# Queries projected with tokens on partitions and turned by DMA, 19 of 20 features a head, and a gram with the keys stationary

## The chip, the cores and the metric

The kernel runs on one core of a Trainium2 chip. The metric is device time in microseconds (us) of one execution. Beside the timed runs there is one profiled execution of the kernel, whose span runs from its first to its last instruction. The core has a matrix engine (TensorE, PE in the profile, with PEld for its loads of stationary operands), a vector engine (DVE), a scalar engine (ACT), GpSimd (POOL), and SyncE (SP), which here only issues DMAs. Each engine runs its own instructions in order and waits on semaphores for the others.

## The reference

x is 2048 tokens by 640 features; there are 32 heads of 20 features. The output mixes a linear attention, whose feature map is a softmax over the 20 features of a head and a softmax of the negated values, with a GEGLU feed-forward of width 1728. The sizes and the function:

```python
    def _A_ref(x, wqkv, w_phi, wo):
...
        qkv = (lambda x, *d: x.transpose(*d))((x @ wqkv).reshape(B, S, 3, H, Dh), 2, 0, 3, 1, 4)
        q, k, v = qkv[0], qkv[1], qkv[2]
        pq = jnp.einsum("bhsd,hdf->bhsf", q, w_phi)
        pk = jnp.einsum("bhsd,hdf->bhsf", k, w_phi)
        phi_q = jnp.concatenate([_softmax(pq, axis=-1), _softmax(-pq, axis=-1)], axis=-1)
        phi_k = jnp.concatenate([_softmax(pk, axis=-1), _softmax(-pk, axis=-1)], axis=-1)
        kv = jnp.einsum("bhsf,bhsd->bhfd", phi_k, v)
        z  = jnp.einsum("bhsf->bhf", phi_k)
        num = jnp.einsum("bhqf,bhfd->bhqd", phi_q, kv)
        den = jnp.einsum("bhqf,bhf->bhq", phi_q, z)[..., None] + 1e-6
        o = num / den
        return (lambda x, *d: x.transpose(*d))(o, 0, 2, 1, 3).reshape(B, S, D) @ wo

    def _B_ref(x, w_gate, w_up, w_down):
        return (_gelu(x @ w_gate) * (x @ w_up)) @ w_down

    x = A_x
    g = _sigmoid((x * gate_w).sum(-1, keepdims=True))
    a = _A_ref(x, A_wqkv, A_w_phi, A_wo)
    b = _B_ref(x, B_w_gate, B_w_up, B_w_down)
    return g * a + (1 - g) * b
```

## The kernel before

All work is written in one order by hand. A small recorder, `_Sched`, gives each operation to its engine in that order and puts in the waits: every operation names the buffers (keys) that it reads and writes, and waits for the last writer of what it reads and for the last writer and all readers of what it writes. A DMA counts as a reader of its source until it has landed. PE never waits for PE. The 16 lanes of SP's queue are used in turn, and a lane waits for its previous DMA.

The tokens are 16 tiles of 128 (`t`), in four blocks of 512 (`b`). The stages:

1. Loads. `loads` (line 208) issues everything on SP: x and the three parts of wqkv, partly by a transposing DMA, and then all feed-forward weights and wo (lines 247 to 257). POOL makes masks and the columns of ones of `vaug`.
2. Folding. `fold` (line 328) multiplies wk and wq by the block-diagonal w_phi, so that pk and pq come straight from x: six matmuls for each 128 rows, and one copy out of PSUM (DVE at line 354, ACT at line 356).
3. Attention state, `attention_state` (line 551). For each token tile: v and pk (`proj`, five matmuls for each stretch of columns, tokens on the partitions), the two exponentials of pk and the gate's exponential on ACT (`k_evac`, lines 423 and 426), the softmax sums, reciprocals and scaling on DVE (`k_norm`, lines 438, 447, 452), and `gram` (line 463), which adds the tile's keys-times-values to PSUM. In the gram the values, 64 columns for three heads, are stationary and 60 key features of both signs are moving; two groups of heads lie side by side in the two column halves of the array. The queries are made for a block of 512 tokens and 128 features at once (`pq`, line 530): the weights are stationary, the 512 tokens moving, so the features come out on the partitions, as the numerators need them; two exponentials (line 537) write them to `Eq`. With `self.columns` set, from the first gram on, `mm` (line 358) writes each matmul as two of 64 stationary columns. The loop over t from 4 to 15 is the main part: k and v of tile t, gram of earlier tiles, and some `pq` units of earlier blocks, in PSUM banks that alternate.
4. The state is turned: `kv_evac` (line 475) copies the gram out and turns it by a DMA (line 494), `kv_mask` (line 509) and `kv_ones` fill `KV`.
5. Feed-forward, `ffn` (line 786). `gateup` (line 640): per block and 128 hidden features, five matmuls of 512 tokens for the gate and five for the up part, gelu on ACT (line 653), product on DVE (line 655). PSUM pairs (0, 1) and (6, 7) alternate. The three last grams stand between the first gateups. `down_pair` (line 716) makes the output of two tiles, with the attention's part added through `goT`.
6. Numerators, `num` (line 671): for each token tile 20 matmuls of 88 columns (four heads), 64 rows each, two at a time in the two row halves of the array; then some small DVE operations, and a transposing DMA (line 713) to `goT`. Tiles 0 and 1 are done between gateups of block 1, the other 14 between downs.

Of the kernel before, what the change touches and what calls it, by code (L numbers as in the profile page):

```python
# [3 lines left out]
P = 128  # L4
# [103 lines left out]
class _Kernel:  # L108
# [13 lines left out]
    NSE = 4  # L122
    NSV = 8
# [8 lines left out]
    def run(self):  # L132
        nc = self.nc
        self.alloc()
        self.columns = False
        self.sc = _Sched(nc, {"sp": (nc.sync, 16), "act": (nc.scalar, 4), "pool": (nc.gpsimd, 2)})
        self.loads()
        self.attention_state()
        self.ffn()
        self.sc.finish(nc.sync)  # L140

    def alloc(self):
# [9 lines left out]
        self.Eq = T("Eq", [P, 2, KD, S], BF16)  # L152
        self.KV = T("KV", [P, KD, 2, self.HB * self.DB], BF16)
        self.hmask = T("hmask", [P, 2, KD, self.HB], BF16)
# [8 lines left out]
        self.hT2 = T("hT2", [P, NFC, BT], BF16)  # L163
        self.wphi_sb = T("wphi_sb", [P, KD, DH], BF16)

        def place(lists):
# [15 lines left out]
            for name, shape, dt, c in plans:  # L182
# [3 lines left out]
            [("w3", [P, KD, 2 * D + 2], BF16), ("wq2", [P, KD, D], BF16)],  # L186
# [3 lines left out]
            [("Ek", [P, self.NSE, 2, D], BF16), ("vaug", [P, self.NSV, self.H, self.DA], BF16),  # L190
             ("Dk", [P, self.NSE, 2, 2 * self.H], F32)],
# [3 lines left out]
            [("xtok", [P, self.TB, D], BF16), ("wkT", [P, KD, D], BF16), ("wqT", [P, KD, D], BF16)],  # L195
            [("goT", [P, 8, KD, P], BF16), ("O1", [P, 2, D], BF16), ("O2", [P, 2, D], BF16),
             ("Og", [P, 2, D], BF16), ("RH", [P, 2, 8, 2, 16], F32), ("outsb", [P, 4, D], BF16)],
# [10 lines left out]
    def loads(self):  # L208
# [34 lines left out]
        half = 7 * P  # L243
        g3 = self.wg.rearrange("(kt p) n -> p kt n", p=P)
        u3 = self.wu.rearrange("(kt p) n -> p kt n", p=P)
        for i, (a, b) in enumerate(((0, half), (half, 13 * P))):
            sc.dma("sp", lambda e, a=a, b=b: e.dma_start(self.wg_sb[:, :, a:b], g3[:, :, a:b]), writes=[("wg", i)])
            sc.dma("sp", lambda e, a=a, b=b: e.dma_start(self.wu_sb[:, :, a:b], u3[:, :, a:b]), writes=[("wu", i)])
            if i == 0:
                sc.dma("sp", lambda e: e.dma_start(self.wgu_sb[:, :, 0:64], g3[:, :, 13 * P:self.F]), writes=["wgu0"])  # L250
                sc.dma("sp", lambda e: e.dma_start(self.wgu_sb[:, :, 64:128], u3[:, :, 13 * P:self.F]), writes=["wgu1"])
        sc.dma("sp", lambda e: e.dma_start(self.wd_sb[:, 0:13, :],
                                           self.wd[0:13 * P, :].rearrange("(c p) n -> p c n", p=P)), writes=["wd"])
        for r in (0, 1):
            sc.dma("sp", lambda e: e.dma_start(self.wd_sb[64 * r:64 * r + 64, 13, :], self.wd[13 * P:self.F, :]),
                   writes=[("wd13", r)])
        sc.dma("sp", lambda e: e.dma_start(self.wo_sb[:, :, :], self.wo.rearrange("(kt p) n -> p kt n", p=P)),
               writes=["wo"])
# [18 lines left out]
        for r in (0, 1):  # L277
            m = self.hmask[:, r, :, :]
            pool(lambda e, m=m: e.memset(m, 1.0), [("hmask", r)])
            pool(lambda e, m=m, r=r: e.affine_select(  # L280
                m, m, pattern=[[4, KD], [-DH, self.HB]], compare_op=ALU.is_ge, fill=0.0, base=-64 * r,
                channel_multiplier=1), [("hmask", r)])
            pool(lambda e, m=m, r=r: e.affine_select(
                m, m, pattern=[[-4, KD], [DH, self.HB]], compare_op=ALU.is_ge, fill=0.0, base=DH - 1 + 64 * r,
                channel_multiplier=-1), [("hmask", r)])
        for s in range(self.NSV):
            pool(lambda e, s=s: e.memset(self.vaug[:, s, :, DH:self.DA], 1.0), [("vone", s)])

# [31 lines left out]
    def gate_column(self, b):  # L320
# [4 lines left out]
        sc.op("dve", lambda e: e.tensor_copy(self.w3[:, :, 2 * self.D:2 * self.D + 1], pv[:, 0:self.KD].unsqueeze(2)),  # L325
              reads=[("ps", b)], writes=["wgate"])

    def fold(self, kt, which, banks, ekey):
# [16 lines left out]
        src = self.pair(banks)  # L345
        if which == "k":
            dst = self.w3[:, kt, self.D:2 * self.D].rearrange("p (b c) -> p b c", c=320)
        else:
            dst = self.wq2[:, kt, :].rearrange("p (i r c) -> p r i c", r=2, c=64)
            src = src.rearrange("p r (i c) -> p r i c", c=64)  # L350
        rd = [("ps", b) for b in banks]
        wr = [("w%s2" % which, kt)]
        if ekey == "d":
            self.sc.op("dve", lambda e: e.tensor_copy(dst, src), reads=rd, writes=wr)
        else:
            self.sc.op("act", lambda e: e.activation(dst, src, AF.Copy), reads=rd, writes=wr)

    def mm(self, bank, c0, n, lhs, rhs, first, fin, reads):

        for a, z in ((0, 64), (64, P)) if self.columns else ((0, P),):  # L360
            self.sc.op("pe", lambda e: e.matmul(  # L361
                self.ps[a:z, bank * 512 + c0:bank * 512 + c0 + n], lhs[:, a:z], rhs, start=first, stop=fin),
                reads=reads, writes=[("ps", bank)], signal=fin and z == P)
# [27 lines left out]
    def k_early(self, t, b0):  # L391
        self.proj(t, 640, 384, b0, 128, ["wk2"])
        self.proj(t, 1024, 257, b0 + 1, 0, ["wk2", "wgate"])
        self.k_evac(t, b0)

    def v_early(self, t, b0):
        self.proj(t, 0, 512, b0, 0, ["wv"])
        self.proj(t, 512, 128, b0 + 1, 0, ["wv"])
        self.v_evac(t, b0)

    def vk(self, t):
        self.proj(t, 0, 512, 0, 0, ["wv"])
        self.proj(t, 512, 512, 1, 0, ["wv", "wk2"])
        self.proj(t, 1024, 257, 2, 0, ["wk2", "wgate"])
        self.v_evac(t, 0)
        self.k_evac(t, 1)

    def v_evac(self, t, B, ek="a"):
        sv = t % self.NSV
        if ek == "d":  # L410
            self.sc.op("dve", lambda e: e.tensor_copy(
                self.vaug[:, sv, :, 0:self.DH], self.bank(B, self.D).rearrange("p (h d) -> p h d", d=self.DH)),
                reads=[("ps", B), ("ps", B + 1), ("vone", sv)], writes=[("vaug", sv)])
            return
        self.sc.op("act", lambda e: e.activation(
            self.vaug[:, sv, :, 0:self.DH], self.bank(B, self.D).rearrange("p (h d) -> p h d", d=self.DH), AF.Copy),
            reads=[("ps", B), ("ps", B + 1), ("vone", sv)], writes=[("vaug", sv)])

    def k_evac(self, t, b0):
        se = t % self.NSE  # L420
        o = b0 * 512 + 128
        for s, scale in ((0, 1.0), (1, -1.0)):
            self.sc.op("act", lambda e, s=s, scale=scale: e.activation(  # L423
                self.Ek[:, se, s, :], self.ps[:, o:o + self.D], AF.Exp, scale=scale),
                reads=[("ps", b0), ("ps", b0 + 1)], writes=[("Ek", se, s)])
        self.sc.op("act", lambda e: e.activation(  # L426
            self.gcol[:, t:t + 1], self.ps[:, o + self.D:o + self.D + 1], AF.Exp, scale=-1.0),
            reads=[("ps", b0 + 1)], writes=[("gcol", t)])
# [5 lines left out]
    def k_sums(self, t):  # L434
        sc = self.sc
        se = t % self.NSE
        H, DH = self.H, self.DH
        sc.op("dve", lambda e: e.tensor_reduce(  # L438
            self.Dk[:, se, 0, :].rearrange("p (s h) -> p s h", h=H),
            self.Ek[:, se, :, :].rearrange("p s (h d) -> p s h d", d=DH), AX.X, ALU.add),  # L440
            reads=[("Ek", se, 0), ("Ek", se, 1)], writes=[("Dk", se)])

    def k_scale(self, t):
        sc = self.sc
        se = t % self.NSE
        H, DH = self.H, self.DH
        sc.op("dve", lambda e: e.reciprocal(self.Dk[:, se, 1, :], self.Dk[:, se, 0, :]),
              reads=[("Dk", se)], writes=[("Rk", se)])
        for s in (0, 1):
            v = self.Ek[:, se, s, :].rearrange("p (h d) -> p h d", d=DH)  # L450
            r = self.Dk[:, se, 1, s * H:(s + 1) * H].unsqueeze(2).to_broadcast([P, H, DH])
            sc.op("dve", lambda e, v=v, r=r: e.tensor_tensor(v, v, r, ALU.mult),  # L452
                  reads=[("Rk", se)], writes=[("Ek", se, s)])

    def gram_groups(self):

        fe = 3 * self.DH
        for g in range(11):
            u = g // 2
            yield (g, 64 * (g % 2), 3 + u // 4, 2 * fe * (u % 4), min(3 * g * self.DA, self.H * self.DA - 64), fe * g,  # L460
                   min(fe, self.D - fe * g))

    def gram(self, t):
        sc = self.sc
        se, sv = t % self.NSE, t % self.NSV
# [85 lines left out]
    def attention_state(self):  # L551
# [16 lines left out]
        for t in range(4):  # L568
            vs(t, 0)
# [305 lines left out]
```

## Time and profile before

| | us |
|---|---|
| median of 3 runs (286.4 to 286.93) | 286.66 |
| span of the profiled execution | 285.0 |
| PE busy in it | 281.1 |
| DVE busy | 174.4 |
| ACT busy | 105.2 |
| POOL busy | 5.3 |
| loads, first v tiles and folds | 0 to 25 |
| main loop and first gateups | 25 to 84 |
| gateups | 84 to 196 |
| downs, with 14 numerators | 196 to 283 |

The span of the profile is 1.7 us shorter than the median of the runs. "Busy" of PE counts a matmul until its result is out, though the next begins long before that, so a group's mean time of one matmul (379 ns for 512 columns) is not what one adds to the span; the distance between starts (216 ns) is.

### The profile page before, as it was taken

The numbers are of one execution on the slowest core, as the hardware profiler recorded it, in microseconds if no ns is written. First come the engines' busy times: TensorE is split into PE (matmuls) and PEld (weight loads), VectorE is DVE, ScalarE is ACT, GpSimd is POOL, SyncE is SP. The second block draws the span as 40 slices with busy tenths as digits, with TensorE's granted clock in tenths as the row PEclk, the third lists the DMA queues.
The fourth block names the chain that finished last, engine by engine and source line by source line (L and its number), as shares of the span: only waits on it lengthen the run. The fifth ranks groups of instructions, "written<-read, shape, count | busy, mean of one in ns | idle before, by whom it ended". The sixth has DMA issues, their size and how long they took to land.

```text
span 285.0 us, 7066 instructions
## 1 busy us (share of the span) xinstructions
PE 281.1 (99%) x3045; PEld 186.1 (65%) x3060; DVE 174.4 (61%) x352; ACT 105.2 (37%) x200; POOL 5.3 (2%) x36
## 2 busy tenths in 40 slices
PE   8999999999999999999999999999999999999996
PEld 4665799999984444444444444445777777777786
DVE  1459999999976652667242334225883883883801
ACT  4367898667754223222322223221112112112021
POOL 7000000000000000000000000000000000000000
DMA  8999993000002000011000000000233223322421
GB/s 228 225 199 313 361 349 111 2 0 2 2 0 48 0 0 2 2 23 25 0 0 0 2 0 0 0 2 0 26 82 58 50 62 59 70 52 68 71 72 48
DMA packets 36937, 18.67 MB, mean 66 GB/s; under 512 B 28970, under 2 KB 36394, under 8 KB 36906
## 3 DMA queue, kind: packets, MB, share of 16 engines
q1 hardware_dynamic: 36240, 18.19, 26.3%
q8 instruction: 24, 0.39, 0.6%
q10 hardware_dynamic: 666, 0.03, 0.2%
q14 instruction: 7, 0.06, 0.1%
HBM read 9.04 MB, written 2.62 MB: 41 GB/s over the span
## 4 chain that ended last, share of the span: by engine, by line
PE 99%; issue 0%; ACT 0%
PE ps L361 62%; PE ps L737 28%; PE ps L681 2%; PE ps L373 2%; PE ps L468 2%; PE ps L341 1%; PE ps L557 1%; PE ps L298 0%; ACT outsb L750 0%; PE ps L564 0%; PE ps L323 0%
## 5 line engine op out<-in xcount | busy, mean ns | idle before, releaser
L361 PE MATMUL ps<-xT,wg_sb 128*128 128x512 bf16 (+1 forms) x265 | 63.8, 379 | 0.4 <-issue 0.2
L361 PE MATMUL ps<-xT,wu_sb 128*128 128x512 bf16 (+1 forms) x263 | 63.3, 379 | 0.4
L653 ACT ACTIVATE gl<-ps 128x512 bf16<-128x512 f32 x52 | 30.9, 596 | 72.9 <-PE ps L361 70.7
L655 DVE TENSOR_TENSOR hT<-ps,gl 128x512 bf16<-128x512 f32 x39 | 26.6, 689 | 38.8 <-PE ps L361 38.7
L737 PE MATMUL ps<-wd_sb,hT 64*128 64x320 bf16 x648 | 48.5, 296 | 0.0
L361 PEld LDWEIGHTS ps<-xT,wu_sb 128*128 128x128 bf16 (+1 forms) x270 | 26.6, 99 | 29.5
L361 PEld LDWEIGHTS ps<-xT,wg_sb 128*128 128x128 bf16 (+1 forms) x270 | 26.2, 99 | 29.0 <-ACT gl L653 0.2
L361 PE MATMUL ps<-w,xT 128*64 128x512 bf16 (+6 forms) x398 | 41.5, 325 | 0.1
L750 ACT ACTIVATE outsb<-ps,Gm 128x320 bf16<-128x320 f32 (+2 forms) x31 | 14.5, 515 | 72.4 <-PE ps L737 72.4
L737 PEld LDWEIGHTS ps<-wd_sb,hT 64*128 64x128 bf16 x648 | 31.1, 94 | 12.2 <-issue 0.4
L361 PEld LDWEIGHTS ps<-w,xT 128*64 128x64 bf16 (+1 forms) x400 | 35.9, 107 | 4.5
L737 PE MATMUL ps<-wo_sb,goT 64*128 64x320 bf16 (+2 forms) x340 | 26.5, 288 | 0.0
L361 PE MATMUL ps<-xT,wq 128*64 128x512 bf16 (+1 forms) x184 | 26.0, 380 | 0.1
L438 DVE TENSOR_REDUCE Dk<-Ek 128x64 f32<-128x1280 bf16 x16 | 23.7, 1478 | 3.7 <-ACT gcol L426 3.7
L452 DVE TENSOR_TENSOR Ek<-Ek,Dk 128x640 bf16<-128x640 bf16 x32 | 25.0, 821 | 0.6
L708 DVE TENSOR_TENSOR O<-ps,RH 128x640 bf16<-128x640 f32 x32 | 24.7, 815 | 0.0
L423 ACT ACTIVATE Ek<-ps 128x640 bf16<-128x640 f32 x32 | 20.7, 703 | 4.2 <-PE ps L361 4.2
L537 ACT ACTIVATE Eq<-ps 128x512 bf16<-128x512 f32 x40 | 21.6, 607 | 0.6 <-PE ps L361 0.4
L655 DVE TENSOR_TENSOR xT<-ps,gl 128x512 bf16<-128x512 f32 x13 | 9.0, 690 | 18.2 <-PE ps L361 18.2
L737 PEld LDWEIGHTS ps<-wo_sb,goT 64*128 64x128 bf16 x340 | 16.0, 94 | 5.3
L361 PEld LDWEIGHTS ps<-xT,wq 128*64 128x64 bf16 (+1 forms) x185 | 15.4, 108 | 2.9
L737 PE MATMUL ps<-wd_sb,xT 64*128 64x320 bf16 (+2 forms) x270 | 16.0, 269 | 0.0
(71 smaller groups left out, 173.8 us busy)
## 6 DMA issues: line engine op xcount, KB each, us to landing
out_dram<-outsb SPq DMA_DIRECT2D x7, 320.0 KB, 2.3
wd_sb<-in_B_w_down_dram SPq DMA_DIRECT2D x1, 2080.0 KB, 12.9
wg_sb<-in_B_w_gate_dram SPq DMA_DIRECT2D x1, 1120.0 KB, 7.4
wu_sb<-in_B_w_up_dram SPq DMA_DIRECT2D x1, 1120.0 KB, 9.8
wg_sb<-in_B_w_gate_dram SPq DMA_DIRECT2D x1, 960.0 KB, 9.1
wu_sb<-in_B_w_up_dram SPq DMA_DIRECT2D x1, 960.0 KB, 9.3
w<-in_A_wqkv_dram SPq DMA_DIRECT2D x5, 160.0 KB, 3.6
wo_sb<-in_A_wo_dram SPq DMA_DIRECT2D x1, 800.0 KB, 8.5
```

The source lines that it names most:

```text
L361: self.sc.op("pe", lambda e: e.matmul(self.ps[a:z, bank * 512 + c0:bank * 512 + c0 + n], lhs[:, a:z], rhs, start=first, stop=fin), reads=r ...
L373: sc.op("pe", lambda e, c0=c0, n=n, bk=bk, col=col: e.matmul(self.bank(bk)[:, col:col + n], self.xT[:, kt, t * P:(t + 1) * P], self.w3[:, ...
L423: self.sc.op("act", lambda e, s=s, scale=scale: e.activation(self.Ek[:, se, s, :], self.ps[:, o:o + self.D], AF.Exp, scale=scale), reads=[ ...
L438: sc.op("dve", lambda e: e.tensor_reduce(self.Dk[:, se, 0, :].rearrange("p (s h) -> p s h", h=H), self.Ek[:, se, :, :].rearrange("p s (h d ...
L452: sc.op("dve", lambda e, v=v, r=r: e.tensor_tensor(v, v, r, ALU.mult), reads=[("Rk", se)], writes=[("Ek", se, s)])
L468: sc.op("pe", lambda e: e.matmul(self.ps[a:a + 64, b * 512 + c:b * 512 + c + 2 * nf], va[:, lo:lo + 64], self.Ek[:, se, :, f0:f0 + nf], st ...
L537: sc.op("act", lambda e, s=s, scale=scale: e.activation(self.Eq[:, s, i, b * self.BT:(b + 1) * self.BT], self.bank(bank), AF.Exp, scale=sc ...
L653: sc.op("act", lambda e: e.activation(self.gl[:, slot, :], self.bank(banks[0]), AF.Gelu_apprx_tanh), reads=[("ps", banks[0])], writes=[("g ...
L655: sc.op("dve", lambda e: e.tensor_tensor(hT, self.bank(banks[1]), self.gl[:, slot, :], ALU.mult), reads=[("ps", banks[1]), ("gl", slot)], ...
L708: dve(lambda e, o=o, f=f, s=s: e.tensor_tensor(o, V[s][:, :, :, 0:DH], f, ALU.mult), rb + [key(6 + s)], [("O", s, sl)], guard=old)
L737: sc.op("pe", lambda e: e.matmul(self.bank(bk, w), lhs, rhs, start=opens and x == 0, stop=end and not opens, skip_group_check=True), reads ...
L750: sc.op("act", lambda e: e.activation(dst, self.bank(bk, w), AF.Copy, scale=g), reads=rd, writes=wr)
```

## The change

The queries are now made as the keys are: one token tile at a time (`q_tile`), tokens on the partitions, 608 columns. Their exponentials go to a buffer `Eqt` of four slots (`NEQ = 4`, slot `t % 4`), and a transposing DMA on SP turns each tile into `Eq`, features on the partitions. Because a softmax does not change when one value is subtracted from all, the fold subtracts each head's last feature from the others: 19 columns a head are left (`E = 19`), the exponential of the twentieth is the constant 1, and the sums get 1 added. So k has 608 columns and not 640, and so has q; a `fold` now ends in a small ACT copy of the last features (`wref`) and a DVE subtraction. Three heads with both signs make one group of 128 features (60 and 4 unused, twice); there are 11 groups. In the gram the 128 key features of a group are stationary and 63 value columns are moving; the result has the features on the partitions already, so the state needs three masked DVE copies (`kv_state`) and no DMA. The numerators take 11 groups of three heads (66 columns), sign 0 in the upper and sign 1 in the lower row half. `self.columns` is gone. The constant columns of `Ek` and `Eqt` are set by nine POOL memsets at the start; per key tile a POOL copy puts the reciprocals in the twentieth columns. v of a tile is made four tiles ahead of its k. The feed-forward weights but the first halves of gate and up are issued from inside the main loop (`weights(1)` to `weights(6)`), behind the query tiles' DMAs on SP. `hT2` shares its memory with `Eqt`.

```diff
-    NSE = 4
-    NSV = 8
+    NSE = 5
+    NSV = 9
+    NEQ = 4
+    E = DH - 1
+    G = 11
+    HG = 3
+    VO = 167
+    KO = 208
...
-    def fold(self, kt, which, banks, ekey):
+    def fold(self, kt, which, banks):
...
+        self.sc.op("act", lambda e: e.activation(ref, src[:, :, :, self.E], AF.Copy), reads=rd, writes=[("wref", kt)])
+        self.sc.op("dve", lambda e: e.tensor_tensor(
+            dst, src[:, :, :, 0:self.E], ref.unsqueeze(3).to_broadcast([P, 2, 16, self.E]), ALU.subtract),
+            reads=rd + [("wref", kt)], writes=[("w%s2" % which, kt)])
+
+    def strip(self, b):
+
+        c = (b + 1) * 512 + 304
+        self.sc.op("dve", lambda e: e.memset(self.ps[:, c:c + self.E], 0.0), writes=[("ps", b + 1)])
...
+    def v_tile(self, t, b):
+        n = 512 - self.VO
+        self.proj(t, 0, n, b, self.VO, ["wv"])
+        self.proj(t, n, self.D - n, b + 1, 0, ["wv"])
...
+    def exps(self, T, sl, name, b):
+
+        o = b * 512 + self.KO
+        src = self.ps[:, o:o + self.G * self.HG * self.E].rearrange("p (g h f) -> p g h f", h=self.HG, f=self.E)
         for s, scale in ((0, 1.0), (1, -1.0)):
...
+            self.sc.op("act", lambda e: e.activation(dst, src, AF.Exp, scale=scale),
+                       reads=[("ps", b), ("ps", b + 1)], writes=[(name, sl, s)])
+
+    def k_tile(self, t, b):
+        n = 513 - self.KO
+        self.proj(t, self.D, n, b, self.KO - 1, ["wk2", "wgate"])
+        self.proj(t, self.D + n, self.H * self.E + 1 - n, b + 1, 0, ["wk2"])
+        self.exps(self.Ek, t % self.NSE, "Ek", b)
...
+    def q_tile(self, t, b):
+        n = 512 - self.KO
+        for bk, c0, a, z in ((b, self.KO, 0, n), (b + 1, 0, n, self.H * self.E)):
+            for kt in range(self.KD):
+                self.mm(bk, c0, z - a, self.xT[:, kt, t * P:(t + 1) * P], self.wq2[:, kt, a:z], kt == 0,
+                        kt == self.KD - 1, [("xT", t), ("wq2", kt)])
+        sl = t % self.NEQ
+        self.exps(self.Eqt, sl, "Eqt", b)
+        self.sc.dma("sp", lambda e: e.dma_start_transpose(self.Eq[:, :, t * P:(t + 1) * P], self.Eqt[:, sl, :]),
+                    reads=[("Eqt", sl, 0), ("Eqt", sl, 1)], writes=[("Eq", t)])
...
     def k_scale(self, t):
...
+        sc.op("dve", lambda e: e.tensor_scalar(D, D, 1.0, None, op0=ALU.add), reads=[("Dk", se)], writes=[("Dk", se)])
+        sc.op("dve", lambda e: e.reciprocal(R, D), reads=[("Dk", se)], writes=[("Rk", se)])
+        sc.op("pool", lambda e: e.tensor_copy(v[:, :, :, self.E], R3), reads=[("Rk", se)], writes=[("Ekc", se)])
+        sc.op("dve", lambda e: e.tensor_tensor(
+            v[:, :, :, 0:self.E], v[:, :, :, 0:self.E],
+            R3.unsqueeze(3).to_broadcast([P, 2 * self.G, self.HG, self.E]), ALU.mult),
+            reads=[("Rk", se)], writes=[("Ek", se, 0), ("Ek", se, 1)])
...
     def gram(self, t):
...
+        for g in range(self.G):
+            n, b, c = min(w, self.H * self.DA - w * g), 4 + g // 8, w * (g % 8)
+            self.sc.op("pe", lambda e: e.matmul(
+                self.bank(b)[:, c:c + n], self.Ek[:, se, g * P:(g + 1) * P], va[:, w * g:w * g + n],
...
     def attention_state(self):
...
+        f, v, k, q = self.fold, self.v_tile, self.k_tile, self.q_tile
+        v(4, 6)
+        v(5, 0)
+        f(0, "k", (2, 3))
+        f(1, "k", (4, 5))
+        f(2, "k", (6, 7))
+        v(6, 0)
+        f(3, "k", (2, 3))
+        f(4, "k", (4, 5))
+        v(7, 6)
+        self.strip(2)
+        k(0, 2)
+        self.strip(6)
+        f(0, "q", (4, 5))
+        f(1, "q", (0, 1))
+        k(1, 6)
+        self.k_sums(0)
+        f(2, "q", (4, 5))
+        k(2, 2)
+        f(3, "q", (0, 1))
+        f(4, "q", (4, 5))
+        self.strip(0)
+        k(3, 6)
         self.k_scale(0)
...
+        for t in (1, 2, 3):
+            self.k_norm(t)
+        g = 0
         for t in range(4, NT):
...
+            if t + 4 < NT:
+                v(t + 4, 0)
+            k(t, 2)
+            for g in range(g, t - 3 if t < 8 else t - 2):
+                self.gram(g)
+            g = t - 3 if t < 8 else t - 2
+            q(t - 4, 6)
             self.k_norm(t)
...
+            if t < 7:
+                self.weights(t - 3)
+            elif t in (9, 10, 11):
+                self.weights(t - 5)
+            if t + 4 >= NT:
+                q(t, 0)
...
     def num(self, t):
...
+        for g in range(self.G):
+            n = min(w, H * DB - w * g)
             for s in (0, 1):
...
+                a, o = 64 * s, base[s] + w * g
+                sc.op("pe", lambda e: e.matmul(
+                    self.ps[:, o:o + n], self.Eq[a:a + 64, g, t * P:(t + 1) * P], self.KV[a:a + 64, g, 0:n],
...
         def state(idx):
             if idx < 3:
                 self.gram(13 + idx)
             if idx == 2:
-                self.columns = False
-                self.kv_evac()
+                self.kv_state()
                 self.gates()
-                self.kv_ones()
-            if 6 <= idx < 11:
-                self.kv_mask(idx - 6)
```

`weights(4)` is w_down (2080 KB), `weights(5)` its last 64 rows in two DMAs, `weights(6)` wo (800 KB); they follow the query tiles 5, 6 and 7 on SP.

## The prediction

> **What bounds the kernel now.** I read the busy times, then the chain of work that ended last, then PE's waits, then the chain in order of time through the main loop.
>
> ```profile
> PE 281.1 (99%) x3045; PEld 186.1 (65%) x3060; DVE 174.4 (61%) x352; ACT 105.2 (37%) x200; POOL 5.3 (2%) x36
> ...
> PE 99%; issue 0%; ACT 0%
> PE ps L361 62%; PE ps L737 28%; PE ps L681 2%; PE ps L373 2%; PE ps L468 2%; PE ps L341 1%; PE ps L557 1%; PE ps L298 0%; ACT outsb L750 0%; PE ps L564 0%; PE ps L323 0%
> ```
>
> PE is the chain: 99% of it. What counts is the matmul columns it streams and every wait put before them. PE's own waits, all of them:
>
> ```profile
> PE ps L557 <- PEq L860: 0.8, 1, 0.8
> PE ps L361 <- issue: 0.2, 1, 0.2
> ```
>
> So nothing before makes PE wait. One round of the main loop, and the end of the grams:
>
> ```profile
> 60.26 0.22 PE ps L468 x7
> 60.48 0.05 PE ps L361
> 60.53 0.04 PE ps L468
> 60.56 3.73 PE ps L361 x34
> 64.30 0.27 PE ps L468 x8
> ...
> 83.93 0.35 PE ps L468 x10
> 84.28 0.16 issue
> ```
>
> A round is some 4.1 us, of which the gram is 0.31 (0.27 and a piece of 0.04). After the last gram PE goes from 64-column to 128-column operands and loses 0.16 and a little more. By the starts of single matmuls in the trace, 512 columns take 216 ns, 384 take 162, 257 take 109.5, 128 take 55.5: columns / 2.4 + about 2.4 ns. I use that formula below. The groups by shape (busy, mean ns of one, idle before) that the costs below are taken from:
>
> ```profile
> L452 DVE TENSOR_TENSOR Ek<-Ek,Dk 128x640 bf16<-128x640 bf16 x32 | 25.0, 821 | 0.6
> ...
> L361 PEld LDWEIGHTS ps<-xT,wu_sb 128*128 128x128 bf16 x250 | 24.5, 98 | 29.5
> ...
> L438 DVE TENSOR_REDUCE Dk<-Ek 128x64 f32<-128x1280 bf16 x16 | 23.7, 1478 | 3.7 <-ACT gcol L426 3.7
> ...
> L423 ACT ACTIVATE Ek<-ps 128x640 bf16<-128x640 f32 x32 | 20.7, 703 | 4.2 <-PE ps L361 4.2
> ...
> L447 DVE RECIPROCAL Dk<-Dk 128x64 f32<-128x64 f32 x16 | 8.8, 552 | 0.5
> ```
>
> and, from the DMA issues, with the time to landing last:
>
> ```profile
> wd_sb<-in_B_w_down_dram SPq DMA_DIRECT2D x1, 2080.0 KB, 12.9
> ...
> Ek<-Ek SPq DMA_TRANSPOSE x1, 3.4
> ```
>
> **PE's columns.** All terms go against the profiled span, 285.0; the median of the runs is 1.7 above it. Five matmuls for each stretch. v of a tile (345 + 295 columns): 5 x (146.2 + 125.3) = 1.36 us. k (305 + 304): 1.29. q (304 + 304): 1.29. Before, k alone (384 + 257) took 1.36 and v with k (512 + 512 + 257) 2.70, so k saves 8 x 0.07 + 8 x 0.05 = 0.95. The q units before are 100 x 216 ns = 21.57; now 16 x 1.29 = 20.66: 0.9 saved. The losses between operand shapes (0.16 at 84.28, about 0.1 at the first gram) go: 0.3. Together -2.2.
>
> **Gram.** 11 matmuls of 63 columns with 128-column loads. No row has this pair; the nearest in the trace are the folds' 80-column matmuls, also with 128-column loads, 35 ns apart, and the x transposes, whose pairs of 64 columns are 29 ns apart at full clock. 29 gives 0.32 a tile, 35 gives 0.385: 0 to +1.2 us over 16. I take 0, since 63 is nearer 64. The Trainium skill speaks against this edit ("TensorE: Matmul & The Clock Gate", Back-to-back issue gap): with a load for each matmul it gives about 81 ns at 128 columns. By that, as an estimate, the gram would be 11 x 81 = 0.89 us, 9 us more in all. The trace disagrees: 55.5 ns at 128 columns, 35 at 80.
>
> **Numerators.** 11 pairs of 66 columns. Before, 10 pairs of 88 take 0.39 us, 39 ns a pair. At 30 ns a pair it is 0.33: 16 x 0.06 = -1.0. Bounds: -1.0, and +0.6 if a pair stays at 39.
>
> **State.** The copies, the DMA at line 494 and the masks went beside gateups that never waited for them; removing them saves 0. The POOL memsets of 1408 columns cost about 1.2 us each (204 ns for 128, 106 for 7), POOL ends near 21 us, the first Ek slot is set near 11 and needed at 20: 0. Without that cover each would delay the k exponentials by 1.2. The first weights wait behind the query DMAs on SP, yet wg, wu and wgu are issued by about 41 us and used from 78 on: 0.
>
> **Folds.** Each now needs a small ACT copy (about 0.2; a one-column ACT is 186 ns) and then a DVE operation of 608 columns (0.79, from 820 for 640); before, two of the ten went to ACT alone. DVE is the bound here. Setting the order against the banks: v(7) waits for the third fold's copy, 0.4; fold q2 wants banks 4 and 5 from q0, 0.6; q4 stands behind k_sums(0) (1.47) and q2 on DVE, 0.9; the first gram waits 0.1. Sum +2.0, bounds 0.5 and 4 (PE's gap there today is 0.2).
>
> **Normalising.** Per tile: the reduction 1.45, adding 1 about 0.2, the reciprocal 0.56, the product 1.38 to the next start (640 columns take 0.74 start to start), with hand-overs 3.8 us; before 3.6. PE's round is 1.36 + 1.29 + 0.32 + 1.29 = 4.26, so DVE keeps up, but it starts late: k_scale(0) begins near 27 us and ends near 29.4, so tile 5 is ready near 48.5. The loop shortens the gram's distance at t = 8, where gram(5) stands at about 46.8: +1.7. Bounds 0 and 3.5 (a round of 4.0 or more on DVE).
>
> **The query slots.** Here the change adds a wait that decides. `Eqt` has four slots, and q(t) uses slot t % 4. From t = 12 on the loop makes q(t - 4) and then q(t): the same slot. The exponentials of q(12) on ACT must wait until the DMA that turns q(8) has landed; likewise 13 for 9, 14 for 10, 15 for 11. Let iteration 12 start at 0 on PE.
>
> PE: k(12) to 1.29, gram to 1.61, q(8) to 2.90, q(12) to 4.19. ACT writes q(8) by 4.24 (two exponentials start 0.57 apart, the second takes 0.69). SP issues the DMA at 4.30. The like DMA of 10 blocks landed 3.36 after issue, its data taking 1.72; for 11 blocks that is 3.55, so 7.85. But w_down (t = 9), its rest and wo (t = 11) are on the same queue, and today everything on it lands in the order of issue: w_down 6.3 us after the transfer before it, the two small ones 0.85 together, wo 1.85. Iteration 9 starts at -12.8, so q(5) is written by -7.2, issued at -7.1 and through at -4.0; w_down follows it: 6.3 + 0.85 + 1.85 + three turns of 1.9 = 10.7, plus 0.5 to the semaphore: 11.2. ACT then writes q(12), to 12.55.
>
> Behind that wait on ACT stand the exponentials of k(13) and of q(9), and behind them q(9)'s DMA. On PE, q(13) needs the banks of q(12) (0 and 1): it is ready at 7.09 and starts at 12.6, a stall of 5.5. From there each link repeats: k exponentials and gate 1.25, q exponentials 1.27, DMA 3.55, q exponentials of the next tile 1.26: about 7.3 us, against 4.19 of PE work. So q(14) and q(15) lose 3.1 each. Then the first gateup wants bank 0: q(15) ends on PE at 28.4, its exponentials at 34.4: 6.0. Sum 5.5 + 3.1 + 3.1 + 6.0 = +17.7. Without the queue behind the weights the first is 2.2: 14.4. Nothing after it has slack, as PE is the chain.
>
> **The clock.** At the start, after no matmuls, the first 512-column matmuls start 427 ns apart and not 216, up to 4.85 us, some 4 us of half clock: 2 us lost. A 6 us gap just before the gateups may bring that back once: 0 to +2.0; I take 2.0, by the only row of a clock after idling. The gaps inside the chain cost less, since ACT and the DMA set the pace. The Trainium skill ("TensorE: Matmul & The Clock Gate", Part 1) has the clock halved after an idle window of about 3.4 us and back after a busy one, which would be some 1.7 us for the last gap; no row of this trace shows it inside the kernel.
>
> **Sum.** 285.0 - 2.2 - 1.0 + 2.0 + 1.7 + 17.7 + 2.0 = 305.2; with the 1.7, 306.9.
>
> **Rivals.**
> 1. The chain without its queue and without the clock: the weights are through before q(8)'s DMA, as PE's late start also delays it. 285.0 - 3.2 + 3.7 + 14.4 + 1.7 = 301.6. For: w_down moves at 330 GB/s, near its best; against: its 6.3 us alone exceed a round.
> 2. The clock falls in every gap and PE's 4.2 us between become up to 8.4, longer than the link of 7.3: 1.1 in each of three links more, and the last gap: 310.2. Against: three of the gaps are 3.1, shorter than the 4 us of the start.
> 3. The other side: the slot wait is not on the path. It decides from a landing within about 1.2 us of the issue, for then q(12)'s exponentials start when PE has it ready. Then 285.0 - 3.2 + 3.7 + 1.7 = 287.2, or, with folds and normalising covered too, 283.5, which is faster. Against: the fastest turning DMA in the trace, half as large, landed after 2.6.
> 4. The gram's loads are not hidden under 63 columns: at 98 ns a load, 11 make 1.08 a tile, 16 x 0.76 = 12.2 more, 319.1. Against: 35 ns at 80 columns. (By the skill's 81 ns it would be 9 more, 315.9.)
> 5. Each DMA of the chain lands 0.7 later (4.2 is the slowest turn today): 4 x 0.7 more, 309.7.
>
> **Chances.** Forecast 0.66, rival 1 0.14, rivals 2 and 5 together 0.13, rival 4 0.02, rival 3 0.05, half of that faster. The forecast's own range is 303 to 310; with rivals 1, 2 and 5, 300 to 312. What this kernel's measurement can tell from no change is about 0.2%: faster 0.03, within 0.01, slower 0.96.
>
> **What would show it.** PE's waits on ACT line 434 appear, four of them, about 5.5, 3.1, 3.1 and 6.0, on banks 0 and 1; ACT waits for Eq's DMA four times; ACT's k exponentials come late from tile 13 on. PE's share falls near 92%. The gram takes 0.32 a tile, the numerators 0.33. Waits for DVE near 17 to 25 us add to 2.0, one at gram(5) is 1.7. Wrong would be: no wait of ACT on a DMA, or PE idle elsewhere, at v or k banks.

## The result, and the profile after

The changed kernel takes 310.04 us (median of 4 runs, 309.49 to 310.64), the kernel before 286.61 beside it (286.4 to 286.93). The ratio is 1.0802, with a 95% interval of 1.0756 to 1.0847: slower by 8%. The profiled execution spans 308.3 us, 23.3 more than the 285.0 of before.

Three views of the changed kernel's page: the busy times, the throttle's clock in 40 slices of 7.7 us (tenths of full speed), and the chain that ended last, by engine.

```profile
PE 285.3 (93%) x2909; PEld 183.7 (60%) x2922; DVE 172.8 (56%) x335; ACT 104.5 (34%) x197; POOL 44.6 (14%) x63
...
PEclk9999999999695799999999999999999999999999
...
PE 72%; issue 9%; POOL 8%; DMA 4%; ACT 3%; SPq 3%; POOLq 0%; ACTq 0%
```

PE was 99% of the chain and is now 72%. (Not all of the rest is loss: from PE's wait at 49.95 us, for a copy by POOL, the chain steps back along POOL to the start, so POOL's 8% and most of the "issue" share lie ahead of that point, where PE worked beside them.) The trace also has 136 matmul records fewer, and yet PE's busy time rose by 4.2 us. The clock is one reason, at 6, 5 and 7 tenths in the 11th, 13th and 14th slice (77 to 85 and 92 to 108 us); the table below has its cost, 2.7 and 2.0 us. The waits of PE, which were 0.8 and 0.2 before (releaser; us in total, times, longest):

```profile
PE ps L388 <- ACT Eqt L434: 15.1, 4, 5.7
PE ps L369 <- DVE wq L378: 1.3, 2, 0.7
PE ps L388 <- DMA xT<-in_A_x_dram: 1.2, 1, 1.2
PE ps L491 <- POOL Ek L479: 0.9, 1, 0.9
PE ps L527 <- PEq L815: 0.8, 1, 0.8
PE ps L491 <- DVE Ek L480: 0.4, 1, 0.4
```

The first line is the mechanism of the forecast: four waits, for ACT's exponentials of a query tile. One step further back, ACT's row among the waits of all engines says what ACT waited for in its turn:

```profile
ACT Eqt L434 <- DMA Eq<-Eqt: 18.7, 4, 7.1
```

The timeline of ACT, 70 to 102 us, only its query exponentials (start, duration, and in brackets the idle time ahead with its releaser):

```profile
76.09 1.28 ACT L434 ACTIVATE Eqt<-ps 128x627 bf16<-128x627 f32 x2 [7.13 <-DMA Eq<-Eqt]
...
78.45 1.33 ACT L434 ACTIVATE Eqt<-ps 128x627 bf16<-128x627 f32 x2
83.51 1.28 ACT L434 ACTIVATE Eqt<-ps 128x627 bf16<-128x627 f32 x2 [3.73 <-DMA Eq<-Eqt]
...
85.87 1.32 ACT L434 ACTIVATE Eqt<-ps 128x627 bf16<-128x627 f32 x2
91.36 1.28 ACT L434 ACTIVATE Eqt<-ps 128x627 bf16<-128x627 f32 x2 [4.16 <-DMA Eq<-Eqt]
...
93.72 1.33 ACT L434 ACTIVATE Eqt<-ps 128x627 bf16<-128x627 f32 x2
98.73 1.28 ACT L434 ACTIVATE Eqt<-ps 128x627 bf16<-128x627 f32 x2 [3.69 <-DMA Eq<-Eqt]
```

Each bracketed row is one of tiles 12 to 15; the row without a bracket behind it is the tile (9, 10, 11) whose transfer the next bracket waits for. The rows of tiles 12 to 15 stand 7.42, 7.85 and 7.37 us apart, against some 4.2 of PE's own work in a round. The chain of waits, in order of time, walks one such link:

```profile
87.28 3.98 DMA Eq<-Eqt
...
91.94 0.69 ACT Eqt L434
92.64 1.17 ACT Ek L434 x2
93.81 0.06 ACT gcol L443
93.87 1.18 ACT Eqt L434 x2
...
95.12 3.50 DMA Eq<-Eqt
...
98.73 1.29 ACT Eqt L434 x2
100.02 0.51 issue
100.53 0.63 PE ps L388
```

Transfer, exponentials of q(14), of k(15), gate, exponentials of q(11), transfer, exponentials of q(15), and only then the first gateup at 100.53: PE's matmuls are not in this link at all. Last, the clock in stretches of the same time (us, PE busy and number of matmuls, then PEld, DVE, ACT, POOL; granted clock; DMA share; GB/s):

```profile
70.00:77.00 7.00, 1.82 (x23) 1.22 (x20) 5.24 (x6) 0.91 (x2) 3.54 (x2) 0.95 0.75 203
77.00:84.00 7.00, 6.58 (x39) 4.27 (x40) 3.69 (x4) 3.27 (x7) 1.77 (x1) 0.56 0.55 103
84.00:91.00 7.00, 4.94 (x46) 3.36 (x43) 3.69 (x4) 3.19 (x7) 1.77 (x1) 1.00 0.64 105
91.00:97.00 6.00, 2.09 (x10) 1.05 (x10) 2.99 (x4) 3.69 (x7) 0.74 (x1) 0.70 0.44 84
97.00:102.00 5.00, 1.47 (x4) 0.74 (x6) 0.70 (x1) 2.56 (x3) 1.03 (x1) 0.50 0.39 73
102.00:110.00 8.00, 7.94 (x63) 3.98 (x62) 2.51 (x5) 2.25 (x4) 0.00 (x0) 0.90 0.15 28
```

PE is busy for 1.82 of the 7 us from 70 to 77, then works at 0.56 of the clock, is idle again, and starts the gateups at 0.50.

**Where the 23.3 us lie.** The first gateup matmul on record behind the last gram starts at 108.47 us and not at 84.44: 24.0 later. From there to the end of the last matmul it is 197.7 and not 198.4: 0.7 less. By the distances between the starts of matmuls, the 24.0 are:

| | us |
|---|---|
| waits for the query slots, 5.77 + 0.46 + 3.61 + 6.08 | +15.9 |
| half clock after the first of them (304 columns 254 ns apart, not 129), which shortened the second | +2.7 |
| half clock after the third (query matmuls, 0.5) and behind the last (7 gateup matmuls 427 ns apart, 1.5) | +2.0 |
| folds, v(7) and the first gram | +2.5 |
| xT of tiles 6 and 7, landed at 16.10 and not 13.99 | +1.4 |
| gram(5) and the one behind it | +1.0 |
| PE's columns (by the forecast's formula, which the distances bear out) | -2.2 |
| gram, 0.33 a tile and not 0.31 | +0.3 |
| not placed | +0.4 |

### The profile page after: what moved, and what is told of

It is laid out like the page before. It is cut to its first block, busy times and chain, and to the rows that moved or that the text cites. A ratio compares the mean times of both kernels' runs of the same rounds, so it can differ in the third digit from the quotient of the medians.

```text
span 308.3 us, 6908 instructions
## 1 busy us (share of the span) xinstructions
PE 285.3 (93%) x2909; PEld 183.7 (60%) x2922; DVE 172.8 (56%) x335; ACT 104.5 (34%) x197; POOL 44.6 (14%) x63
## 4 chain that ended last, share of the span: by engine, by line
PE 72%; issue 9%; POOL 8%; DMA 4%; ACT 3%; SPq 3%; POOLq 0%; ACTq 0%
PE ps L388 43%; PE ps L695 26%; DMA Eq<-Eqt 4%; POOL Ek L479 3%; ACT Eqt L434 2%; PE ps L640 2%; SPq L455 2%; POOL Ek L285 2%; POOL Eqt L287 2%; PE ps L491 1%; SPq L297 1%; ACT Ek L434 1%; POOL vaug L283 0%; POOL mask L261 0%; POOL mask L264 0%
## 5 line engine op out<-in xcount | busy, mean ns | idle before, releaser
L388 PE MATMUL ps<-xT,wg_sb 128*128 128x512 bf16 x250 | 64.3, 383 | 6.2 <-ACT Eqt L434 5.7
L388 PE MATMUL ps<-xT,wu_sb 128*128 128x512 bf16 x257 | 65.0, 382 | 0.2
L388 PEld LDWEIGHTS ps<-xT,wg_sb 128*128 128x128 bf16 x260 | 25.2, 98 | 36.0 <-issue 6.7
L388 PEld LDWEIGHTS ps<-xT,wu_sb 128*128 128x128 bf16 x260 | 25.7, 99 | 31.5 <-issue 1.4
L388 PE MATMUL ps<-w,xT 128*128 128x305 bf16 (+3 forms) x280 | 41.5, 302 | 1.2 <-DMA xT<-in_A_x_dram 1.2
L479 POOL CAST Ek<-Dk 128x66 bf16<-128x66 f32 x16 | 28.3, 1772 | 51.5 <-DVE Dk L478 47.7
L388 PEld LDWEIGHTS ps<-w,xT 128*128 128x128 bf16 x280 | 27.2, 99 | 12.3 <-DMA xT<-in_A_x_dram 1.4
L388 PE MATMUL ps<-wq,xT 128*128 128x304 bf16 x160 | 25.0, 308 | 9.4 <-ACT Eqt L434 9.4
L468 DVE TENSOR_REDUCE Dk<-Ek 128x66 f32<-128x1254 bf16 x16 | 23.2, 1453 | 10.9 <-ACT gcol L443 10.9
L480 DVE TENSOR_TENSOR Ek<-Ek,Dk 128x1254 bf16<-128x1254 bf16 x16 | 23.5, 1468 | 0.5
```

Of the source, the lines that this page charges most:

```text
L388: self.sc.op("pe", lambda e: e.matmul(self.ps[:, bank * 512 + c0:bank * 512 + c0 + n], lhs, rhs, start=first, stop=fin), reads=reads, writ ...
L468: self.sc.op("dve", lambda e: e.tensor_reduce(self.Dk[:, se, 0, :].rearrange("p (u h) -> p u h", h=self.HG), self.k_view(se)[:, :, :, 0:se ...
L479: sc.op("pool", lambda e: e.tensor_copy(v[:, :, :, self.E], R3), reads=[("Rk", se)], writes=[("Ekc", se)])
L480: sc.op("dve", lambda e: e.tensor_tensor(v[:, :, :, 0:self.E], v[:, :, :, 0:self.E], R3.unsqueeze(3).to_broadcast([P, 2 * self.G, self.HG, ...
```

## The experiments

Nine kernels ran. The table at the end of this part has all their times.

**The slot, taken away.** The slots are handed out in the order in which the tiles are made (q(8), q(12), q(9), q(13) ...), so that no tile takes the slot of the one just before it.

```diff
-        sl = t % self.NEQ
+        sl = self.qn % self.NEQ
+        self.qn += 1
```

> The slots of Eqt are given out in the order in which the query tiles are made, so q(12) takes another slot than q(8). Theory (the slot wait is the cause): PE's four waits on ACT line 434 (5.8, 0.5, 3.6 and 6.1 us between starts) go, the first gateup starts 16.3 us earlier (at about 84.3, since q(12) ends at 71.65 and three rounds of 4.19 follow), and the half-speed stretch at its start (7 x 0.21 = 1.5) goes: 310.0 - 17.8 = 292.2 us. Rival (the turning DMAs themselves, behind the weights, are too slow for the loop): PE still waits on line 434 and the time stays above 300 us.

Measured: 290.23 us, 1.0125 [1.011, 1.014] of before. The order of four slots is worth 19.8 us, 2.0 more than expected. The expectation took 71.65 us for the end of q(12) on PE; it is that of q(9), one tile of 1.29 and two rounds before the gateups and not three rounds. By starts the table's 15.9, 2.7 and 2.0 go and a wait of 1.73 stays, 18.9 together; xT, landing at 15.32 in this profile and not at 16.10, gives most of the rest. Its waits of PE:

```profile
PE ps L388 <- ACT Eqt L434: 1.6, 1, 1.6
PE ps L369 <- DVE wq L378: 1.3, 2, 0.7
PE ps L492 <- POOL Ek L480: 0.9, 1, 0.9
...
```

Of four waits for the query exponentials one is left, ahead of the first gateup, which shares bank 0 with q(15). The profile gives a granted clock of 1.0 for the whole span, and no two gateup matmuls stand further apart than at full clock. The slot is the cause of the loss, and with it of the clock's fall.

**The queue behind the weights.** The changed kernel, with w_down, its rest and wo issued after the loop.

```diff
-            elif t in (9, 10, 11):
-                self.weights(t - 5)
...
+        for n in (4, 5, 6):
+            self.weights(n)
```

> The changed kernel with w_down, its rest and wo issued after the last query tile, so that no weights stand before q(8)'s DMA; the slots are as changed. Theory: q(8)'s DMA lands 3.5 us after its issue and not 5.9, and is issued earlier as well (69.2 and not 70.1), so the first wait falls from 5.8 to about 2.4 and the others stay: 306.6 us. Rival A (the clock that falls in the first gap costs its 2.7 us beside the wait): 304. Rival B (the queue behind the weights is not what made the first wait long): 310.

Measured: 305.18 us, 1.0645 [1.0627, 1.0663]. ACT's timeline in it shows the first of the four brackets:

```profile
73.60 1.28 ACT L434 ACTIVATE Eqt<-ps 128x627 bf16<-128x627 f32 x2 [3.69 <-DMA Eq<-Eqt]
...
80.97 1.28 ACT L434 ACTIVATE Eqt<-ps 128x627 bf16<-128x627 f32 x2 [3.68 <-DMA Eq<-Eqt]
```

It is 3.69 where it was 7.13, and the link, 7.37, is as long as before (7.42). By starts, PE's waits are 2.3, 3.1, 2.0 and 6.2, together 13.7: the forecast's price without the queue was 14.4. So 3.5 us of the first wait (5.8 to 2.3) were the weights ahead of q(8)'s transfer: 2.4 because it landed 5.9 us after its issue and here 3.5, and 1.0 because SP, which had issued wo just ahead of it, came to it that much later against PE's work (1.56 us before the end of q(9) on PE, here 2.61). The time lies between the theory's 306.6 and rival A's 304, and this run doesn't tell them apart: the profiled execution, 306.89, is itself 1.7 above the median, with 1.1 of waiting for wk at the first folds, and here the clock stayed full behind the first wait and fell behind the second.

**The clock.** The changed kernel, with 18 matmuls on data that nobody uses, ahead of the first gateup; they run within the wait.

```diff
+        for n in range(18):
+            sc.op("pe", lambda e: e.matmul(self.bank(2), ones[:, 0:P], ones[:, 0:512], start=True, stop=True),
+                  writes=[("ps", 2)])
```

> The changed kernel with 18 more matmuls of 512 columns on constants into bank 2, whose results nothing uses, between the last query tile and the first gateup, where PE waits for 6.1 us. Theory (the wait lets the clock fall to half, and the first gateups pay for it): the first gateup matmuls come 216 ns apart and not 427, 7 x 0.21 = 1.5 us less: 308.5 us. Rival (the slow matmuls there have another cause, or the wait before was all there is to win): 310 us or more.

Measured: 307.72 us, 1.0735 [1.0715, 1.0755], 2.3 less than the changed kernel. In the stretch that holds its first gateups the clock is full:

```profile
90.00:100.00 10.00, 7.36 (x31) 3.55 (x32) 3.69 (x4) 5.68 (x10) 1.77 (x1) 0.83 0.38 72
100.00:104.00 4.00, 4.00 (x29) 2.00 (x28) 0.69 (x1) 1.76 (x3) 0.00 (x0) 1.00 0.48 90
```

No pair of gateup matmuls is 427 ns apart any more. That accounts for 1.5 us of the 2.3; in this profile xT also came earlier (waits of 0.6 in place of 1.4), which is as much as the rest.

**gram(5).** The kernel with slots in order, and the gram kept four tiles behind throughout, its twelfth after the loop.

```diff
-            for g in range(g, t - 3 if t < 8 else t - 2):
+            for g in range(g, t - 3):
                 self.gram(g)
-            g = t - 3 if t < 8 else t - 2
+            g = t - 3
...
+        self.gram(12)
```

> As e1_order, and the gram stays four tiles behind the keys to the end (gram(12) after the loop), where the changed kernel goes from four to three at t = 8. Theory (gram(5) came before tile 5 was scaled, by 1.0 us): e1_order less 1.0: 291.2 us. Rival (DVE, being late, only moves the wait to a later gram): the same as e1_order, 292.2.

Measured: 289.58 us, 1.0112 [1.0087, 1.0138], 0.65 less than with the slots alone. The wait at gram(5) is gone, but part of what it gave came back ahead of the first gateup, where PE now waits 2.46 us by starts and not 1.73. The chain of this kernel, in order of time, at the first gateup, and the clock in stretches around it:

```profile
74.41 5.58 DMA Eq<-Eqt
...
80.69 0.70 ACT Eqt L434
...
81.52 2.56 PE ps L388 x7
```

```profile
79.00:82.00 3.00, 0.69 (x10) 0.36 (x8) 2.90 (x5) 1.89 (x3) 1.77 (x1) 1.00 0.95 205
82.00:84.00 2.00, 2.00 (x7) 0.76 (x6) 1.90 (x4) 1.27 (x2) 0.32 (x1) 0.54 1.27 203
```

q(15) has the slot of q(13). A PE that comes earlier finds q(13)'s transfer still out, which landed at 79.99, 5.6 us after its issue, and ACT late with q(15): PE waits 2.5 us for bank 0. In this profile the clock then halves for seven matmuls (1.5 us), behind the first three gateup matmuls at full clock. That cost is not in the median: the profiled execution took 290.88 at a mean granted clock of 0.994, the other three 289.34 to 289.63 at 1.0.

**The loads at the start.** xT(6, 7) landed 2 us later than before in the changed kernel's profile. The diff puts nine memsets on POOL there, so this kernel (slots in order) holds those of the key and query buffers until xT(6) has landed.

```diff
-            pool(lambda e, s=s: e.memset(self.Ek[:, s, :], 1.0), [("Ek", s, 0), ("Ek", s, 1), ("Ekc", s)])
+            pool(lambda e, s=s: e.memset(self.Ek[:, s, :], 1.0), [("Ek", s, 0), ("Ek", s, 1), ("Ekc", s)],
+                 reads=[("xT", 6)])
```

> As e1_order, but POOL's nine long memsets of Ek and Eqt start only when x tiles 6 and 7 have landed. In every kernel with these memsets so far the turning DMA of x tiles 6 and 7 landed late (15.0 to 17.1 us, against 13.99 before the change), and PE waited 0.2 to 1.4 us for it at the first fold or v tile 6. Theory (the memsets slow the loads beside them): landing at about 14.0, no wait of PE there: 0.6 less than e1_order, 289.6 us. Rival (the loads differ by themselves from run to run): landing as late as before, 290.2.

Measured: 292.23 us, 1.0185 [1.0158, 1.0211], more than either side expected, and xT(6, 7) landed at 16.67, not earlier. As far as one profile can tell, the idea that the memsets hold the loads falls. Of the 2.0 us over e1, this profile has, by starts, 1.6 as a wait of the first folds for wk, which landed at 15.27 (e1: 13.46), and 0.8 as a longer wait ahead of the first gateup. That wait, 2.53 us, is as long as the one in e4, yet the clock stayed full (the last part says why). Over the profiles of all ten changed kernels this landing lies between 14.8 and 17.1 us, with the same loads in the same order; before had 13.99 in its one profile. What moves it stays open.

**The end of the loop.** Three answers to what e4 showed: slots in order and gram four behind, the late weights of e2, and the gateups' bank pairs begun with (6, 7) in place of (0, 1), which q(15) holds.

```diff
-        self.pn = 0
+        self.pn = 1
```

> As e4_lag, with the three late weight transfers after the last query tile (as in e2_late_weights) and the first gateup on banks 6 and 7, not on banks 0 and 1 that q(15) has just used. Theory (what is left of the wait before the first gateup, 2.5 us, is ACT waiting for turning DMAs behind the weights, 0.6 and 1.2 us, plus the evacuation of the same banks, and it brings the half clock for 7 matmuls, 1.5 us): both go: 289.6 - 4.0 = 285.6 us. Rival (DMA turns of two tiles a round are too slow by themselves): the wait stays above 1 us and the time above 288.

Measured: 287.51 us, 1.0032 [1.0019, 1.0044]. No wait for a query slot or its banks is left:

```profile
PE ps L369 <- DVE wq L378: 1.3, 2, 0.7
PE ps L528 <- PEq L818: 0.8, 1, 0.8
PE ps L400 <- DMA w<-in_A_wqkv_dram: 0.5, 1, 0.5
PE ps L492 <- DVE Ek L481: 0.4, 1, 0.4
PE ps L492 <- POOL Ek L480: 0.3, 1, 0.3
PE ps L388 <- DMA xT<-in_A_x_dram: 0.2, 1, 0.2
```

It missed 285.6 by 1.9, though. Of the 4.0 us that the expectation took off e4's median, 1.5 was the half clock that only e4's profiled execution had; without it the sum is 287.1. Left at the start are the two waits of the query folds (0.82 and 0.83 by starts) and the first gram's (0.59), which stand as they were; 0.44 stands at the last gram, for its tile's normalising.

**The start, put in another order.** As e6, with the query folds further apart and the gram behind the query tile of its round.

```diff
         k(1, 6)
         self.k_sums(0)
-        f(2, "q", (4, 5))
         k(2, 2)
+        f(2, "q", (4, 5))
         f(3, "q", (0, 1))
+        k(3, 6)
         f(4, "q", (4, 5))
         self.strip(0)
-        k(3, 6)
         self.k_scale(0)
...
             k(t, 2)
+            q(t - 4, 6)
             for g in range(g, t - 3):
                 self.gram(g)
             g = t - 3
-            q(t - 4, 6)
```

> As e6_tail, with the query folds moved apart (fold q2 after k(2), fold q4 after k(3)) and each gram after the query tile of its round and not before it. Theory (three waits for DVE, 0.8 at fold q2, 0.8 at fold q4 and 0.6 at gram(0), are a matter of order): two of them and the most of the third go, 1.9 less than e6_tail: 283.7 us. Rival (DVE is the bound of the start, so the waits only move to the next user): the same as e6_tail.

Measured: 288.24 us, 1.0057 [1.004, 1.0074]: the rival was right, nothing was gained. The fold waits became 0.82 and 0.38 and the first gram's is gone, but a new one of 0.72 stands at v(8), behind a memset by DVE that sits behind the folds, and the last gram's grew from 0.44 to 1.09. Together they are 3.0, where e6 had 2.7. A new order moves waits about; what is short is DVE.

**The start, with less work on DVE.** The softmax's constant may be taken off w_phi just as well as off the folded weights: one subtraction on a small matrix in place of ten large ones, and a fold is one copy again, which ACT may take.

```diff
     def blockdiag(self):
+        d = self.wphi_sb[:, :, 0:E]
+        self.sc.op("dve", lambda e: e.tensor_tensor(
+            d, d, self.wphi_sb[:, :, E:E + 1].to_broadcast([P, self.KD, E]), ALU.subtract),
...
...
-    def fold(self, kt, which, banks):
+    def fold(self, kt, which, banks, ekey):
...
-        self.sc.op("act", lambda e: e.activation(ref, src[:, :, :, self.E], AF.Copy), reads=rd, writes=[("wref", kt)])
-        self.sc.op("dve", lambda e: e.tensor_tensor(
-            dst, src[:, :, :, 0:self.E], ref.unsqueeze(3).to_broadcast([P, 2, 16, self.E]), ALU.subtract),
+        if ekey == "d":
+            sc.op("dve", lambda e: e.tensor_copy(dst, src), reads=rd, writes=wr)
+        else:
+            sc.op("act", lambda e: e.activation(dst, src, AF.Copy), reads=rd, writes=wr)
```

> As the run with the short tail (e6, 287.51 us), with the subtraction of a head's last feature made once, in w_phi, before the block-diagonal matrix is built; each of the ten folds then has one copy out of PSUM (three of the k folds and all five of the q folds on VectorE, two k folds on ScalarE) in place of a copy by ScalarE and a subtraction by VectorE behind it. Theory: what is left of the loss before the first gateup is VectorE's work in the start, its subtractions above all (waits of the two q folds of .82 and .83 us and of gram(0) of .59 in e6). Those waits should go or shrink to under .3 each: about 285.4 us, under the 286.6 of before. Rival: as when only the order was changed (e7, 288.24), the waits only move to the next thing that VectorE makes: 287.5 us, same as e6. A second rival: the extra operation on w_phi comes late, behind the load of w_phi, and holds the first fold: a wait of .5 us or more at the first fold, 287.5 to 288.

> As e8, with the copy of the last q fold on ScalarE in place of VectorE. Theory: it takes some .6 us from VectorE just ahead of gram(0): 284.8 us, with gram(0)'s wait under .2 us. Rival: ScalarE is then late with its own next work, the copies of k and xT, and nothing is gained over e8: 285.4 us or more.

Measured: 285.46 us, 0.9955 [0.9943, 0.9967], and with the last query fold on ACT 284.94 us, 0.9942 [0.9927, 0.9957]. Both beat the kernel before, by about half a percent. The intervals overlap, so the second step alone isn't shown. PE's waits, and the groups of DVE's folds (busy, mean ns, idle ahead), in the last kernel:

```profile
PE ps L532 <- PEq L822: 0.8, 1, 0.8
PE ps L392 <- DMA xT<-in_A_x_dram: 0.7, 1, 0.7
PE ps L373 <- DVE wq L382: 0.2, 1, 0.2
...
```

```profile
L382 DVE CAST wq<-ps 128x608 bf16<-128x608 f32 x4 | 3.0, 787 | 0.7 <-PE ps L373 0.7
L382 DVE CAST w<-ps 128x608 bf16<-128x608 f32 x3 | 2.3, 792 | 4.2 <-PE ps L373 4.2
```

A copy takes DVE as long as the subtraction did (787 ns, against 785 in e6); what DVE was spared is three of the ten (two in e8), and a fold no longer has a small copy by ACT ahead of it. These runs don't tell which of the two did it. The folds' two waits became one of 0.4 by starts, and the first gram's is gone. With the last gram's, the waits went from 2.7 in e6 to 0.6 in e8, as much as the time fell.

| kernel | us | ratio to before |
|---|---|---|
| the change | 310.04 | 1.0802 |
| e3: the change, array kept busy | 307.72 | 1.0735 |
| e2: the change, late weights | 305.18 | 1.0645 |
| e5: slots in order, held memsets | 292.23 | 1.0185 |
| e1: slots in order | 290.23 | 1.0125 |
| e4: e1, gram four behind | 289.58 | 1.0112 |
| e7: e6, start reordered | 288.24 | 1.0057 |
| e6: e4, late weights, other banks first | 287.51 | 1.0032 |
| e8: e6, subtraction on w_phi | 285.46 | 0.9955 |
| e9: e8, last fold on ACT | 284.94 | 0.9942 |

## Why the prediction was right, step by step

310.04 is 1% above the forecast of 306.9. It lies at the very edge of the forecast's own range (303 to 310) and inside the wider one (300 to 312), and the numbers of rivals 2 (310.2) and 5 (309.7) come nearer to it. The number alone wouldn't decide for the forecast; its steps do, each beside a measurement. Rival 5 fell, for behind the first the chain's transfers landed after 3.54, 3.98 and 3.50, where 3.55 was put; rival 1 fell with e2, and rivals 3 and 4 with the four waits and the gram's 32 ns.

- **The query slots, +17.7.** Right in place, number and cause (e1). The link was put at 7.3 and is 7.42, 7.85 and 7.37. The four waits were put at 5.5, 3.1, 3.1 and 6.0; measured 5.8, 0.5 with 2.7 of half clock beside it, 3.6 and 6.1. Together 18.6, 0.9 more than the forecast: half of it in the middle link, whose transfer took 3.98 and not 3.55.
- **The queue behind the weights, 3.3 of these.** Right (e2: 3.5). The transfer was thought to land 6.9 after its issue and did so after 5.9.
- **The clock, +2.0.** Right in sum, and that by luck: the last gap, for which all of it was put, cost 1.5 (e3 takes it away), and 0.5 more came after the third wait, for which nothing was put. Rival 2 was half right in its mechanism: the clock fell in the first gap and again just behind the third, and not in the last alone. It wasn't right in its price, for it rose again before the round was over: after the first wait PE's round took 6.96 us and not 8.4, a little less than the link of 7.42, so the link set the pace just as at full clock.
- **Folds, +2.0.** Right in kind, small by 0.5: v(7) 0.2 for 0.4, the query folds 0.8 and 0.8 for 0.6 and 0.9, the first gram 0.6 for 0.1. That it was DVE's work and not the banks' order was shown by e7 and e8.
- **Normalising, +1.7.** At its place, gram(5), but 1.0. The tile's period on DVE is 3.70, for 3.8; the first tile was thought done at 29.4 and was at 31.3, as its scaling began at 28.65 and not near 27, behind the late load and the folds. PE came later to gram(5) too, by 2.2 (48.95 for 46.8).
- **Gram 0, numerators -1.0.** The gram's 63-column matmuls with a load each are 32 ns apart, between the two rows that bounded them (29 and 35): +0.3. The 81 ns of the Trainium skill ("TensorE: Matmul & The Clock Gate", Back-to-back issue gap) didn't come about, nor rival 4. The numerators came to 0.35 a tile by starts, where 0.33 was put, on the 14 tiles between the downs from 0.39: -0.6, and all behind the last gram -0.7.
- **POOL's memsets and the moved state, 0.** No wait stands there.
- **A misread row.** The 0.16 lost at 84.28, a part of the 0.3 for operand shapes (and the 0.2 among PE's waits before), is mostly a matmul without a record: two weight loads of the first gateup stand at 84.21 and 84.225, but its first matmul on record at 84.44, 216 ns later, which is the time of one. The loss there is about 0.1; for the sum this is nothing.
- **Not in the sum: the load of xT, +1.4.** The step that put no price on the loads, because their order doesn't change, took one profile's landing for a constant. This term and the slots' 0.9 are the larger part of the 3.1 us between forecast and result.

Whether late weights or other banks would also help the kernel before wasn't tried; nothing in its profile waits for them.

## What to carry to other kernels

When a ring of buffers is indexed by the tile's number, write down the order in which tiles are made: two that follow each other must not get the same slot, or every transfer out of it becomes a link of the chain. If PE is 99% of the chain, any such link is paid in full, and a gap of a few us may be paid again in clock. Where an engine is short of time in one stage, moving work about in that stage only moves the waits (e7); doing the arithmetic earlier, on the small operand, takes them away (e8).

## What the runs showed of the hardware

- **The clock changes on a grid of 3.41 us, and a gap shorter than that can be enough.** The granted clock of the changed kernel, in windows set to where it changes:

```profile
72.89:76.31 3.42, 0.00 (x0) 0.00 (x0) 2.38 (x4) 0.22 (x1) 1.77 (x1) 1.00 0.84 220
76.31:83.13 6.82, 5.71 (x32) 3.62 (x33) 3.69 (x4) 3.47 (x7) 1.77 (x1) 0.50 0.56 106
83.13:93.37 10.24, 6.49 (x60) 4.54 (x58) 3.69 (x4) 5.70 (x11) 1.77 (x1) 1.00 0.44 72
```

  The half-clock stretch of the second row and the full one of the third last 2 and 3 times 3.41 us, and the half-clock stretch behind them (93.37 to 103.61) 3 times. In e2 the half-clock stretches last 3.41 and 6.83, in e3 6.83 and 3.41, in e4 3.41. So it matters where in the grid a gap falls. The 2.46 us of e4 (79.0 to 81.5) lay inside one step (78.74 to 82.15), and the clock fell at its end, when PE was at work again; the 2.53 us of e5 (81.8 to 84.5) lay across a border (83.53), and it stayed full. (Two other executions of e5 have a mean granted clock of 0.994, as much as one step at half.) The 1.73 us of e1 brought no fall. The 3.6 us in the changed kernel ended at 92.69, and the clock fell at 93.37. Worked out from the starts and columns of the matmuls (columns / 2.4 ns each, twice that at half clock) in the profiles of the changed kernel and e2 to e5, PE streamed for at most 35% of each step that a fall followed, and for at least 42% of each step behind which the clock stayed full (the nearest: 35 and 31% in e2 and 26% in e4 with a fall, 42% in e2 and 53% in e5 without). The Trainium skill ("TensorE: Matmul & The Clock Gate", Part 1) gives a free-running window of 3413 ns, so that the point of the change depends on where in it the work falls. The trace agrees in the 3.41; but the page's table asks for an idle window ahead of a fall, and the one in e4 was not idle throughout.
- **A tiny copy on GpSimd beside VectorE.** The copy of 66 elements took 1.77 us all 16 times, as the profile has it (its spans on POOL are rough):

```profile
L479 POOL CAST Ek<-Dk 128x66 bf16<-128x66 f32 x16 | 28.3, 1772 | 51.5 <-DVE Dk L478 47.7
```

  It starts each time with DVE's product of the same tile (29.54 and 29.51, for one) and ends 0.33 us after it, so it is ready last, and is what gram(5) waits for. The Trainium skill ("GPSIMD Engine Reference", Specifications) says that the two share their SBUF interfaces and collide when VectorE has two SBUF inputs, as this product does; no run had the copy without the product beside it, so this isn't shown.
- **The same loads land differently.** Between 14.8 and 17.1 us for one transfer, over ten profiles: 1 us at the start of such a kernel is not to be read from a single one.
